# Two of three exponent shifts from DVE to GpSimd, singly allotted shift buffers, a packed output projection and one query map, in a statically scheduled attention kernel

## The chip, the cores and the metric

The kernel runs on one core of one Trainium2 chip. The metric is device time in microseconds (us); for the profiled run of the kernel before it was 802.34 us, 1.8 us more than the span from the first to the last instruction that its profile shows. One core has PE (TensorE, matmuls), DVE (VectorE), ACT (ScalarE), GpSimd (written POOL in the profile) and SP, which here only starts DMA transfers. "Clock" is the mean TensorE clock that the profile shows as granted, as a share of full speed. Runs that are more than 1.5% slower than the fastest of the same kernel are marked slow; the ratios below use only the fast ones.

## The reference

Two independent layers share the launch; the outputs lie side by side.

```python
# A: multi-query attention, S=2048, D=512, H=32 heads of Dh=16, one shared key and value head
q = (x @ wq) as [H, S, Dh];  k = x @ wk;  v = x @ wv
p = softmax(q @ k.T * Dh**-0.5);  a = concat_heads(p @ v) @ wo
# B: linear attention
q, k, v = x @ wqkv, by head
phi(t) = concat(softmax(t @ w_phi), softmax(-(t @ w_phi)))     # per head
o = (phi(q) @ (phi(k).T @ v)) / (phi(q) @ sum(phi(k)) + 1e-6);  b = o @ wo
out = concat(a, b, axis=-1)
```

What matters is the exponential in A: 32 heads x 2048 x 2048 scores. In blocks of 128 keys by 512 queries, four of which make a "quad", that is 512 quads. Two engines can turn a quad of scores in PSUM into exponentials, and both are used at once.

## The kernel before

The first way is ACT: `exp` out of PSUM, two or three blocks at a time. The second is DVE, which builds the exponential out of float16 bits. One instruction per block (a "conversion") scales the score and writes it as int16, so that the bits, read as float16, are a rough power of two. Three more copies of the quad are this one plus 256, 512 and 768 (the "shifts": 256 is a quarter of an exponent step). PE then sums all four copies, each with its own weight K in the value matrix VK; the weighted sum is a better exponential.

```python
# kernel before, cut
def bits():                       # "dz": one of 4 blocks of a quad, PSUM -> SBUF
    o = Z[:, 0, h, :]             # Z: 3 quad buffers x 4 copies x 4 blocks x 512, int16
    v.tensor_scalar(out=o, in0=ps[:, bank, :], scalar1=self.Z1, scalar2=self.Z0, op0=ALU.mult, op1=ALU.add)
def shift(t):                     # "dS": t = 1, 2, 3, all on DVE
    v.tensor_scalar(out=Z[:, t], in0=Z[:, 0], scalar1=256.0 * t, scalar2=None, op0=ALU.add)
def d_pv(quad):                   # "dpv": one PE job of 16 matmuls, after all three shifts
    for k in range(4):
        for g in range(4):
            pe.matmul(ps[32 * g:32 * g + 32, bank, :], lhsT=w[:, k, :], rhs=Zf[:, k, sl[g], :],
                      start=start and k == 0, stop=stop and k == 3, tile_position=(0, 32 * g))
```

The order of instructions on every engine is fixed before launch. A planner on the host lists jobs with durations measured earlier, issues the job that can start first, and thereby fixes each engine's queue and how many quads DVE takes. On the chip the engines are held together only by semaphores, and a semaphore is set only where one instruction reads or overwrites data of another. The planner decides freely how many quads DVE takes. It also puts filler matmuls on constant data into PE gaps when its count of recent PE activity is low.

```python
def weight(self, j):              # PE activity of a job, cut
    if j.mode == "row": return 0.28 * (self.gsize[j.name[1]] if k == "qk" else 1)
    if j.mode == "col": return 0.41 if k == "kv" else 0.68 if k == "pv" else 2.7     # 2.7: "dpv", 16 matmuls
# in run(): if n >= 2 and te > 14 and self.active(s) < self.ACTIVE: ... issue a filler
```

Of the kernel before, what the change touches and what calls it, by code (L numbers as in the profile page):

```python
# [1159 lines left out]
class _Fast:  # L1160
# [13 lines left out]
    NQ = 3  # L1174

    def __init__(self, nc, st, ins, out):
# [22 lines left out]
        self.Z = sb("Z", [128, self.NQ, 4, 4, 512], I16)  # L1199
        self.onesK = sb("onesK", [128, 4, 32], BF)  # L1200
        self.bmx = sb("bmx", [128, 64], F32)
        self.On = sb("On", [128, 12, 512], BF)
        self.wo_pad = sb("wo_pad", [128, 8, 512], BF)
# [10 lines left out]
        self.Wq = sb("Wq", [128, 4, 2, 16, 2, 16], BF)  # L1214
# [4 lines left out]
        self.Ek = sb("Ek", [128, 2, 32, 2, 16], BF)  # L1219
        self.vS = sb("vS", [128, 2, 32, 2, 17], BF)  # L1220
# [4 lines left out]
        self.KVs = sb("KVs", [128, 8, 2, 2, 4], BF)  # L1225
# [17 lines left out]
        self.fin = 0.0  # L1243
# [50 lines left out]
    def ready(self, j):  # L1294

        if j.keys is None:
            self.rec = []
            j.fn()
            j.keys = ({r for _, rs, _ in self.rec for r in rs}, {w for _, _, ws in self.rec for w in ws if w != ("PS", None)})
            self.rec = None  # L1300
        t = j.rel
        rs, ws = j.keys
        for m, kk in ((self.tw, rs | ws), (self.tr, ws)):
            for k in kk:
                if k in m:
                    f, e = m[k]
                    if e != j.eng:
                        f += self.SEM
                    elif e == "pe":
                        f = 0.0  # L1310
                    t = max(t, f)
        if j.nb:
            fr = sorted(max(self.tr.get(("PS", b), (0.0,))[0], 0.0) + self.SEM for b in self.free)
            if len(fr) < j.nb:
                return None
            t = max(t, fr[j.nb - 1])
        return t

    def issue(self, j, start):
# [11 lines left out]
        self.te[j.eng] = max(self.te[j.eng], start + dur)  # L1331
        self.fin = start + dur + self.TAIL[j.eng]
# [78 lines left out]
    def head(self):  # L1411
# [23 lines left out]
        for k in range(4):  # L1435
            add("pool", (lambda k: (lambda g: g.memset(self.VK[:, k, :, 16:32], self.K[k])))(k), writes=[("VK1", k)])
            add("pool", (lambda k: (lambda g: g.memset(self.onesK[:, k, :], self.K[k])))(k), writes=["onesK"])
        add("pool", lambda g: g.memset(self.denS, 1.0), writes=[("denS", 0), ("denS", 1)])
        add("pool", lambda g: g.memset(self.bmx, 0.0), writes=["bmx"])
        if True:  # L1440
# [10 lines left out]
            add("pool", lambda g: g.memset(self.wo_pad, 0.0), writes=["wo_pad0"])  # L1451
            S.batch_begin("sp")
            for g in range(4):
                for e in range(2):
                    srcw = self.A_wo.rearrange("(A g e d) n -> g e d A n", A=4, g=4, e=2)[g, e]
                    dstw = self.wo_pad[32 * g:32 * g + 16, e:8:2, :]
                    S.dma((lambda s_, d_: (lambda q: q.dma_start(d_, s_)))(srcw, dstw), reads=["wo_pad0"], writes=["wo_pad"])
            S.batch_end()
# [11 lines left out]
            for a in range(2):  # L1470
                o = self.KVs[:, :, 0, a, :]
                add("pool", (lambda a, o: (lambda g: g.tensor_copy(out=o, in_=mask[:, 1 - a, :].unsqueeze(1).to_broadcast([128, 8, 4]))))(a, o),
# [9 lines left out]
        for k, t in (("wk_rep", 3.5), ("half1", 3.0), ("wv", 8.2), ("wq", 8.2), ("VA1", 5.0), ("ones", 1.0), ("zero", 1.0), ("bmx", 14.0)):  # L1482
# [11 lines left out]
    def jobs_a(self):  # L1494
# [16 lines left out]
        for qt in range(12):  # L1511
            qc = qt // 4
            for h in range(2):
                job(("op", qt, h), "pe", 0.87, (lambda qt, h: (lambda: self.outproj(qt, h)))(qt, h), mode="full", nb=1 - h, prio=3.5 - 2.6 * h,
                    after=[("on", qc * 8 + a) for a in range(4 * h, 4 * h + 4)] + ([("op", qt, 0)] if h else [("on", qc * 8 + 7)]))
            job(("oa", qt), "dve", 0.60, (lambda qt: (lambda: self.outproj2(qt)))(qt), after=[("op", qt, 1)], frees=[("op", qt, 0)], prio=1)
        for i in range(4):
            for h in range(2):
                job(("pp", i, h), "pe", 0.87 if h == 0 else 0.44, (lambda i, h: (lambda: self.out_part(i, h)))(i, h), mode="full", nb=1 - h, prio=3.5 - 2.6 * h,
                    after=[("on", 24 + a) for a in range(6)] + [("bk", 15), ("bv", 15)] + [("bq", 3, G) for G in range(8)] + ([("pp", i, 0)] if h else []))  # L1520
            job(("ppc", i), "dve", 0.60, (lambda i: (lambda: self.out_part2(i)))(i), after=[("pp", i, 1)], frees=[("pp", i, 0)], prio=1)
        for sc in range(31):
            job(("rc", sc), "dve", 0.18, (lambda sc: (lambda: self.finish_sc2(sc)))(sc), after=[("ac", sc)], prio=1.1)
            job(("on", sc), "dve", 0.60, (lambda sc: (lambda: self.finish_sc3(sc)))(sc), prio=1.3,
                after=[("rc", sc)] + ([("op", 4 * ((sc - 12) // 8) + i, (sc - 12) % 8 // 4) for i in range(4)] if sc >= 12 else []))
# [136 lines left out]
    def sums(self, sc):  # L1662

        start, stop = self.ndone[sc] == 0, self.ndone[sc] == 15
        if self.rec is None:
            self.ndone[sc] += 1
# [9 lines left out]
    def pv(self, q):  # L1676
# [4 lines left out]
        start, stop = self.sums(sc)  # L1681
# [19 lines left out]
    def dq_ok(self):  # L1701
        if self.dbusy > self.DBUSY or self.dz_out >= self.NOUT or self.dn // 4 - self.NQ >= self.dpvq:
            return False
        return self.dn % 4 != 0 or self.dve_quad() is not None

    def next_dq(self):
# [3 lines left out]
        p = quad % self.NQ  # L1710
        Z = self.Z[:, p]

        def scores():
            if self.rec is None:
                if h == 0:
# [3 lines left out]
                    self.dleft = [0, 1, 2, 3]  # L1719
                sc, kap = self.dquads[quad]  # L1720
# [13 lines left out]
        def bits():  # L1734
            bank, ps = self.bank(("dq", k)), self.ps
            o = Z[:, 0, h, :]
            self.add("dve", lambda v: v.tensor_scalar(out=o, in0=ps[:, bank, :], scalar1=self.Z1, scalar2=self.Z0, op0=ALU.mult, op1=ALU.add),  # L1737
                     reads=[("PS", bank)], writes=[("Z", p, h)])
            if self.rec is None:
                self.dz_out -= 1  # L1740
                self.dbusy += 1.2 if h == 3 else -0.6
        self.job(("dq", k), "pe", 0.22, scores, mode="row", nb=1, prio=1.0, ok=self.dq_ok)
        self.job(("dz", k), "dve", 0.60, bits, after=[("dq", k)], frees=[("dq", k)], prio=1.2)
        if h < 3:
            return
        zk = [("Z", p, x) for x in range(4)]

        def shift(t):
            def go():
                self.add("dve", lambda v: v.tensor_scalar(out=Z[:, t], in0=Z[:, 0], scalar1=256.0 * t, scalar2=None, op0=ALU.add),  # L1750
                         reads=zk, writes=[("Zt", p, t)])
                if self.rec is None:
                    self.dbusy -= 0.6
            return go
        for t in range(1, 4):
            self.job(("dS", quad, t), "dve", 0.60, shift(t), after=[("dz", k - x) for x in range(4)], prio=2)
        self.job(("dpv", quad), "pe", 0.87, lambda: self.d_pv(quad), mode="col", prio=1.4,
                 after=[("dS", quad, t) for t in range(1, 4)] + [("va", x) for x in range(4)], ok=lambda: self.acc_ok(self.dquads[quad][0]))

    def d_pv(self, quad):  # L1760
# [3 lines left out]
        p = quad % self.NQ  # L1764
        Zf = self.Z[:, p].bitcast(F16)
        start, stop = self.sums(sc)
        rd = [("VK", k, kap // 4) for k in range(4)] + [("VK1", k) for k in range(4)] + ["onesK"]
        rd += [("Z", p, h) for h in range(4)] + [("Zt", p, t) for t in range(1, 4)]
        todo = [(self.ACC, self.VK[:, :, kap, :])] + ([(self.den_bank, self.onesK)] if sc == 31 else [])
        for bank, w in todo:  # L1770
            def fn(pe, bank=bank, w=w):
                mm = None
                for k in range(4):
                    for g in range(4):
                        mm = pe.matmul(ps[32 * g:32 * g + 32, bank, :], lhsT=w[:, k, :], rhs=Zf[:, k, sl[g], :],  # L1775
                                       start=start and k == 0, stop=stop and k == 3, tile_position=(0, 32 * g))
                return mm
            kw = dict(writes=[("PS", bank)]) if start else dict(accum=[("PS", bank)])
            self.add("pe", fn, reads=sorted(set(rd), key=str), **kw)
        if self.rec is None:  # L1780
            self.dpvq += 1
# [33 lines left out]
    def finish_sc3(self, sc):  # L1815
        r, qc, a = sc % 2, sc // 8, sc % 8
        accS, R, On = self.accS, self.denS, self.On
        self.add("dve", lambda v: v.tensor_tensor(out=On[:, sc % 12, :], in0=accS[:, r, :], in1=R[:, r, :], op=ALU.mult),  # L1818
                 reads=[("accS", r), ("denS", r), ("row", r)], writes=[("On", sc % 12)])

    def outproj(self, qt, half):
# [3 lines left out]
        bank = self.bank(("op", qt, 0))  # L1825
        q0 = (qt % 4) * 128

        def fn(pe):
            mm = None
            for a in range(4 * half, 4 * half + 4):  # L1830
                mm = pe.matmul(ps[:, bank, :], lhsT=On[:, (8 * qc + a) % 12, q0:q0 + 128], rhs=self.wo_pad[:, a, :], start=(a == 0), stop=(a == 7))  # L1831
            return mm
        kw = dict(writes=[("PS", bank)]) if half == 0 else dict(accum=[("PS", bank)])
        self.add("pe", fn, reads=[("On", (qc * 8 + a) % 12) for a in range(4 * half, 4 * half + 4)] + ["wo_pad", "wo_pad0"], **kw)

    def outproj2(self, qt):
        ps, oa = self.ps, self.outA
        bank = self.bank(("op", qt, 0))
# [6 lines left out]
    def out_part(self, i, half):  # L1845
        ps, On = self.ps, self.On
        bank = self.bank(("pp", i, 0))
        lo, hi = (0, 4) if half == 0 else (4, 6)

        def fn(pe):  # L1850
            mm = None
            for a in range(lo, hi):
                mm = pe.matmul(ps[:, bank, :], lhsT=On[:, a, i * 128:i * 128 + 128], rhs=self.wo_pad[:, a, :], start=(a == 0), stop=(a == 5))
            return mm
        kw = dict(writes=[("PS", bank)]) if half == 0 else dict(accum=[("PS", bank)])
        self.add("pe", fn, reads=[("On", a) for a in range(lo, hi)] + ["wo_pad", "wo_pad0"], **kw)

    def out_part2(self, i):
        bank = self.bank(("pp", i, 0))
        self.copy(self.part[:, i, :], self.ps[:, bank, :], [("PS", bank)], [("part", i)] + [("BxT", c) for c in range(4)])  # L1860

    def finish_last(self):
# [8 lines left out]
        def last(i, a):  # L1871
            def fn(pe):
                return pe.matmul(ps[:, i, :], lhsT=self.On[:, a, i * 128:i * 128 + 128], rhs=self.wo_pad[:, a, :], start=(a == 6), stop=(a == 7))
# [483 lines left out]
```

## Time and profile before

The kernel took 797.5 us (median of the first three runs) and 800.25 us with one run more. The profiled run spans 800.5 us.

The table of busy time, kernel before: busy us, share of the span, number of instructions.

```profile
PE 754.1 (94%) x7457; PEld 246.6 (31%) x7457; DVE 727.9 (91%) x1261; ACT 746.9 (93%) x688; POOL 17.2 (2%) x49
```

The costliest groups, kernel before: line, engine, operation, output<-input, shapes and count, then busy us in total, mean ns of one, and idle time just before.

```profile
L1645 ACT ACTIVATE f_PT<-f_ps 128x1536 bf16<-128x1536 f32 x619 | 719.5, 1262 | 36.4 <-PE f_ps L1590 33.0
L1737 DVE TENSOR_SCALAR f_Z<-f_ps 128x512 int16<-128x512 f32 x500 | 326.6, 681 | 28.5 <-PE f_ps L1590 28.1
L1750 DVE TENSOR_SCALAR f_Z<-f_Z 128x2048 int16<-128x2048 int16 x375 | 247.8, 684 | 1.1
L1396 PE MATMUL f_ps<-f_ones,f_zero 128*128 128x512 bf16 (+9 forms) x229 | 65.9, 354 | 2.0 <-POOL f_zero L1415 1.3
```

ACT's exponentials (L1645), DVE's conversions (L1737) and shifts (L1750) fill their two engines; GpSimd is empty. 500 conversions are 125 quads on DVE; the other 387 are ACT's. The last line is the fillers, matmuls on constant data that the planner puts into PE gaps.

### The profile page before, as it was taken

To read this page: it belongs to the slowest core of one execution; us is meant where nothing else is said; L and a number is where in the kernel's file an instruction comes from. 1 tells how busy PE (TensorE), PEld (TensorE's weight loads), DVE (VectorE), ACT (ScalarE), POOL (GpSimd) and SP (SyncE) were. 2 spreads that over 40 slices of the span, in tenths; PEclk is the share of its full clock that TensorE was granted. 3 is DMA by queue.
4 is the path that set the end of the run, shared out by engine and by line. 5 is a ranking of instruction groups with operands and counts; after the bars stand their busy time and mean duration, and the time that the engine had idled before them with its cause. 6 is when DMAs were issued, how large, how long until landed. Compare 5 with 4: busy or idle time off the path is not lost.

```text
span 800.5 us, 17448 instructions
## 1 busy us (share of the span) xinstructions
PE 754.1 (94%) x7457; PEld 246.6 (31%) x7457; DVE 727.9 (91%) x1261; ACT 746.9 (93%) x688; POOL 17.2 (2%) x49
## 2 busy tenths in 40 slices
PE   8999999999999999999999999999999999989995
PEld 2323222333233233333333333333223333333332
DVE  3799999999899999997989898999899989999954
ACT  3999998999899999999999999999899999999972
POOL 5000000000000000011000000000000000000000
PEclk9999999999799999999999999999899999999999
DMA  6561111110111110111101111110111111011111
GB/s 133 111 129 9 9 7 8 8 8 4 6 8 21 22 8 4 7 9 8 9 4 19 35 7 9 21 15 10 6 9 21 22 21 19 11 9 15 21 14 37
DMA packets 45181, 17.12 MB, mean 21 GB/s; under 512 B 37092, under 2 KB 43236, under 8 KB 45096
## 3 DMA queue, kind: packets, MB, share of 16 engines
q1 hardware_dynamic: 45096, 15.93, 16.0%
q8 instruction: 60, 0.98, 0.5%
q14 instruction: 25, 0.20, 0.1%
HBM read 2.15 MB, written 4.19 MB: 8 GB/s over the span
## 4 chain that ended last, share of the span: by engine, by line
DVE 64%; PE 26%; ACT 4%; DMA 3%; SPq 2%; issue 1%; POOL 0%; DVEq 0%; POOLq 0%
DVE f_Z L1737 26%; DVE f_Z L1750 19%; PE f_ps L1590 8%; PE f_ps L1775 4%; PE f_ps L1687 4%; ACT f_PT L1645 4%; PE f_ps L2084 3%; DVE f_vS L2033 2%; DVE f_ssum L2007 2%; PE f_ps L1396 2%; DVE f_On L1818 2%; DVE f_Wk L2144 2%; DVE f_accS L1402 2%; PE f_ps L1831 1%; DMA f_denS<-f_denS 1%
## 5 line engine op out<-in xcount | busy, mean ns | idle before, releaser
L1645 ACT ACTIVATE f_PT<-f_ps 128x1536 bf16<-128x1536 f32 x619 | 719.5, 1262 | 36.4 <-PE f_ps L1590 33.0
L1737 DVE TENSOR_SCALAR f_Z<-f_ps 128x512 int16<-128x512 f32 x500 | 326.6, 681 | 28.5 <-PE f_ps L1590 28.1
L1590 PE MATMUL f_ps<-f_QA,f_KR 32*128 32x512 bf16 x2048 | 314.4, 389 | 24.2 <-DVE f_Z L1737 13.5
L1750 DVE TENSOR_SCALAR f_Z<-f_Z 128x2048 int16<-128x2048 int16 x375 | 247.8, 684 | 1.1
L1590 PEld LDWEIGHTS f_ps<-f_QA,f_KR 32*128 32x128 bf16 x2048 | 80.1, 91 | 256.0 <-ACT f_PT L1645 87.9
L1687 PE MATMUL f_ps<-f_PT,f_VA 128*32 128x512 bf16 x1548 | 152.5, 393 | 0.7 <-DVE f_accS L1402 0.2
L1775 PE MATMUL f_ps<-f_Z,f_VK 128*32 128x512 f16 x2000 | 133.3, 387 | 3.7 <-DVE f_Z L1750 1.7
L1396 PE MATMUL f_ps<-f_ones,f_zero 128*128 128x512 bf16 (+9 forms) x229 | 65.9, 354 | 2.0 <-POOL f_zero L1415 1.3
L1687 PEld LDWEIGHTS f_ps<-f_PT,f_VA 128*32 128x32 bf16 x1548 | 38.1, 93 | 93.5 <-issue 82.7
L1775 PEld LDWEIGHTS f_ps<-f_Z,f_VK 128*32 128x32 bf16 x2000 | 42.9, 96 | 64.5 <-DVE f_Z L1750 14.3
L2084 PE MATMUL f_ps<-f_BxT,f_Wq 128*128 128x512 bf16 x128 | 33.2, 382 | 1.6 <-DVE f_Z L1737 1.0
L1396 PEld LDWEIGHTS f_ps<-f_ones,f_zero 128*128 128x128 bf16 (+2 forms) x229 | 17.7, 97 | 33.2 <-issue 21.7
L1831 PE MATMUL f_ps<-f_wo_pad,f_On 128*128 128x512 bf16 x96 | 24.9, 382 | 0.6 <-DVE f_Z L1737 0.6
L2144 DVE TENSOR_TENSOR f_Wk<-f_ps,f_wq 128x512 bf16<-128x512 f32 x32 | 21.7, 681 | 2.7 <-PE f_ps L2133 2.7
L1818 DVE TENSOR_TENSOR f_On<-f_accS,f_denS 128x512 bf16<-128x512 f32 x31 | 21.2, 682 | 1.3 <-DMA f_denS<-f_denS 1.2
L1402 DVE COPY f_accS<-f_ps 128x512 f32<-128x512 f32 x31 | 21.2, 684 | 1.1 <-PE f_ps L1687 1.0
L2091 ACT ACTIVATE f_ET<-f_ps 128x512 bf16<-128x512 f32 x32 | 20.8, 649 | 0.6 <-PE f_ps L2084 0.5
L1542 DVE TENSOR_SCALAR f_KR<-f_ps,f_half 128x512 bf16<-128x512 f32 x8 | 5.6, 746 | 15.8 <-PE f_ps L1534 15.8
L2033 DVE TENSOR_TENSOR f_vS<-f_ps,f_rs 128x1024 bf16<-128x1024 f32 x16 | 19.6, 1222 | 0.0
L2001 ACT ACTIVATE f_Ek<-f_ps 128x512 bf16<-128x512 f32 x32 | 17.7, 622 | 1.8 <-PE f_ps L1993 1.7
L2007 DVE TENSOR_REDUCE f_ssum<-f_Ek 128x64 f32<-128x1024 bf16 x16 | 19.4, 1212 | 0.0
L2174 PE MATMUL f_ps<-f_Bwo,f_oT 128*128 128x512 bf16 x64 | 16.6, 382 | 2.2 <-DVE f_Z L1737 1.2
(95 smaller groups left out, 325.9 us busy)
## 6 DMA issues: line engine op xcount, KB each, us to landing
f_denS<-f_denS SPq DMA_DIRECT2D x124, 30.0 KB, 3.0
out_dram<-f_outB SPq DMA_DIRECT2D x18, 128.0 KB, 1.9
f_denC<-f_accS SPq DMA_DIRECT2D x124, 2.0 KB, 1.7
f_denS<-f_denC SPq DMA_DIRECT2D x124, 2.0 KB, 1.7
out_dram<-f_outA SPq DMA_DIRECT2D x14, 128.0 KB, 2.2
f_wq<-in_A_wq_dram SPq DMA_DIRECT2D x1, 512.0 KB, 4.0
f_Bwv<-in_B_wqkv_dram SPq DMA_DIRECT2D x1, 512.0 KB, 5.3
f_Bwo<-in_B_wo_dram SPq DMA_DIRECT2D x1, 512.0 KB, 9.3
```

Source lines behind the costliest of these rows:

```text
L1396: mm = pe.matmul(ps[0:m, bank, 0:n].rearrange("p (a n) -> p a n", n=128), lhsT=zero[0:r, 0:m], rhs=rhs, start=start, stop=start, **kw)
L1402: self.add("dve", lambda v: v.tensor_copy(out=out, in_=in_), reads=reads, writes=writes)
L1590: return pe.matmul(self.ps[:, bank, :], lhsT=self.KR[32 * g:32 * g + 32, sc % 2, kap * 128:(kap + 1) * 128], rhs=self.QA[32 * g:32 * g + 3 ...
L1645: self.add("act", lambda a: a.activation(out=PT[:, sl[0]:sl[0] + size, :], in_=ps[:, b0:b0 + size, :], func=ACT.Exp), reads=[("PS", b0 + i ...
L1687: mm = pe.matmul(ps[32 * g:32 * g + 32, bank, :], lhsT=w, rhs=PT[:, slots[g], :], start=start, stop=stop, tile_position=(0, 32 * g))
L1737: self.add("dve", lambda v: v.tensor_scalar(out=o, in0=ps[:, bank, :], scalar1=self.Z1, scalar2=self.Z0, op0=ALU.mult, op1=ALU.add), reads ...
L1750: self.add("dve", lambda v: v.tensor_scalar(out=Z[:, t], in0=Z[:, 0], scalar1=256.0 * t, scalar2=None, op0=ALU.add), reads=zk, writes=[("Z ...
L1775: mm = pe.matmul(ps[32 * g:32 * g + 32, bank, :], lhsT=w[:, k, :], rhs=Zf[:, k, sl[g], :], start=start and k == 0, stop=stop and k == 3, t ...
L1818: self.add("dve", lambda v: v.tensor_tensor(out=On[:, sc % 12, :], in0=accS[:, r, :], in1=R[:, r, :], op=ALU.mult), reads=[("accS", r), (" ...
L2033: self.add("dve", lambda v: v.tensor_tensor(out=vS[:, :, :, 0:16], in0=v3, in1=rs.unsqueeze(3).to_broadcast([128, 32, 2, 16]), op=ALU.mult ...
L2084: mm = pe.matmul(ps[:, bank, :], lhsT=w[:, dc].rearrange("p x h a f -> p (x h a f)")[:, G * 128:G * 128 + 128], rhs=xT[:, dc, m * 512:(m + ...
L2144: self.add("dve", lambda v: v.tensor_tensor(out=o, in0=i, in1=w.unsqueeze(3).to_broadcast([128, 2, 16, 16]), op=ALU.mult), reads=[("PS", b ...
```

## The change

Its intent is to free DVE. Two of the three shifts of a quad go to GpSimd, as int32 adds of two packed int16 values. The Z memory is the same size but allotted as 12 single copies instead of 3 quads, and the quad's product on PE is split into four jobs, one for each copy. The planner treats the access of GpSimd adds, DVE shifts ("dS") and DVE output scalings ("on") to the on-chip memory SBUF as one resource, which this text calls the port: it plans no GpSimd add while a shift or a scaling is planned, nor the reverse. On PE, the output projection is packed to half the matmuls by a DMA that moves odd heads to free partitions, and B's query map is computed once and exponentiated with both signs. The diff, cut; `...` marks what is left out:

```diff
-        self.Z = sb("Z", [128, self.NQ, 4, 4, 512], I16)          # NQ = 3
+        self.Z = sb("Z", [128, self.NZ, 4, 512], I16)             # NZ = 12
+        self.step = sb("step", [128, 2, 2], I16)                  # 512, 512 and 768, 768
@@ ready(), issue(): the shared port as a resource of the plan
+        if j.eng == "pool" or j.name[0] in self.LOCK:
+            t = max(t, self.te_port)
...
+        if j.eng == "pool" or j.name[0] in self.LOCK:
+            self.te_port = start + dur
@@ shifts
-                self.add("dve", lambda v: v.tensor_scalar(out=Z[:, t], in0=Z[:, 0], scalar1=256.0 * t, scalar2=None, op0=ALU.add),
-                         reads=zk, writes=[("Zt", p, t)])
+                if eng == "dve":
+                    fn = lambda v: v.tensor_scalar(out=Z[:, z], in0=Z[:, z0], scalar1=256.0 * t, scalar2=None, op0=ALU.add)
+                else:
+                    a, b = (Z[:, x].rearrange("p h n -> p (h n)").bitcast(I32) for x in (z0, z))
+                    c = self.step[:, t - 2, :].bitcast(I32).to_broadcast([128, 1024])
+                    fn = lambda g: g.tensor_tensor(out=b, in0=a, in1=c, op=ALU.add)
+                self.add(eng, fn, reads=zk, writes=[("Z", z)] + [("Zp", z, x) for x in range(4)])
+        for t in (3, 2, 1):
+            left = max(self.te["pool"] - self.fin, 0.0) + self.PSHIFT * self.pooled
+            eng = "pool" if t > 1 and left < self.PLEFT[3 - t] else "dve"
@@ the product: one job for each copy
-        self.job(("dpv", quad), "pe", 0.87, lambda: self.d_pv(quad), mode="col", prio=1.4,
-                 after=[("dS", quad, t) for t in range(1, 4)] + ...)
+        for t in range(4):
+            self.job(("dpv", quad, t), "pe", 0.22 if sc < 31 else 0.43, ... self.d_pv(quad, t) ..., mode="col", prio=1.4,
+                     after=([("dS", quad, t)] if t else []) + ...)
+    PSHIFT = 1.95
+    PLEFT = (4.0, 2.0, 0.0)
+    LOCK = ("dS", "on")
@@ output projection, odd heads moved by DMA; 4 matmuls instead of 8
+        if r:
+            for g in range(4):
+                dst = self.On[32 * g + 16:32 * g + 32, p % 6, :] ...   # <- self.Ot, 16 partitions
-            for a in range(4 * half, 4 * half + 4):
+            for A in range(4):
@@ query map: half the matmuls, two exponentials each
-    def b_eq(self, m, G):
-        ... activation(out=self.ET[:, sl, :], in_=self.ps[:, bank, :], func=ACT.Exp)
+    def b_eq(self, m, G, a):
+        ... activation(out=self.ET[:, sl, :], in_=self.ps[:, bank, :], func=ACT.Exp, scale=1.0 - 2.0 * a)
... (layouts of Ek, vS, KVn, KVs follow; the function weight() is not touched)
```

## The prediction

> **What bounds it now.** Three engines share one softmax and all are full. The table of busy time gives PE 754.1 us (94%), ACT 746.9 (93%), DVE 727.9 (91%), GpSimd 17.2 (2%) of 800.5. In the table of stretches ACT and DVE are 95-99% busy from 60 to 760 us. Of 512 score quads, ACT takes 387 (719.5 us in the groups, 1.86 us each) and DVE 125. A DVE quad costs four bit conversions out of PSUM (326.6 us) and three 128x2048 int16 shifts (247.8 us): 4.6 us. The chain of waits is 45% these two DVE lines. PE is near its limit but not at it: about 58 us of its busy time between 20 and 780 us are filler matmuls on ones and zeros.
>
> **What changes.** Two of three shifts go to GpSimd as 128x1024 int32 adds. A DVE quad falls to about 3.3 us (4 x 0.653 + 0.661). Balance: ACT 1.86(512-n) + 27 = DVE 3.27n + 151 + about 15 of port waits gives n near 158 quads on DVE, about 685 us on each, against 747/728. The 53 us during which ACT is not busy (mostly the first and last 20 us) stay: ideally 738 us.
>
> PE: one query map saves 64 matmuls (half of 33.2 us), packed output projection about half of 24.9 + 6.6 + 2.1 us: some 33 us busy. About 33 more DVE quads cost PE 12 more matmuls each (about 0.65 us, from 16 in 0.87 us), some 21 us. So PE work is about level, in less time: fillers shrink, PE waits take part of the gain. ACT work for the query map is unchanged. Four more transfers per pair of heads lie off the chain (DMA share about 12%).
>
> **What it may cost.** GpSimd time of one add: no such instruction is in this trace; the change's planner says 1.95 us; the 2-input add in the skill's table (GPSIMD Engine Reference, Performance versus the Vector engine: 4497 ns for 2048) halves to an estimate of 2.25 us. SBUF — State Buffer, "Who interferes with whom", says a GpSimd instruction and a DVE instruction in a 2-port mode, or with two SBUF inputs, exclude each other. The port then carries about 2 x 1.95 + 0.66 = 4.6 us per quad, over 700 us for 158 quads: nearly full. The plan models this for shifts and output scaling, so some shifts stay on DVE (I expect 1.7-1.9 per quad on GpSimd), but not for the small SBUF-only DVE instructions (about 40). No run here shows this yet. Expected loss over ideal: 10-25 us.
>
> **Prediction: 757 us, 80% range 738 to 788; faster by over 2% 0.82, within 2% 0.13, slower 0.05.**
>
> **What would show it.** Bit conversions rise from 500 to 600-650; exponentials fall from 619 to about 575 at the same 1.26 us mean; DVE shifts fall from 375 to 160-210; GpSimd shows 260-310 adds of about 2 us, busy 70-80%; query-map matmuls 128 to 64, output projection 96 to 48; ACT and DVE still over 90%, PE too. Port conflict would show as DVE shifts with mean well over 0.68 us, small SBUF-only DVE instructions likewise, and waits of PE and DVE on GpSimd adds.
>
> **What would make it wrong.** If an add takes 2.3 us or more, the static order lags behind GpSimd and everything waits on it: time near 790-800. If port blocking is smaller and PE follows well, 740. If splitting the quad's product into four PE jobs adds many row/column mode switches, PE becomes the bound, with DVE and ACT idle on PE scores: 770-785.

## More of the kernel before

A small DVE instruction that will matter, in the groups kept apart by shape:

```profile
L2013 DVE TENSOR_TENSOR f_bmx<-f_ssum,f_bmx 128x64 f32<-128x64 f32 x16 | 3.6, 222 | 0.0
```

The times of the plan are not enforced.

## The result, and the profile after

The changed kernel took 883.12 us (median of 4; the two fast runs 872.56 and 879.45, the two slow ones 886.79 and 891.49), against 800.25 us for the kernel before. The ratio of the fast runs is 1.0948 (95% interval 1.0827 to 1.1069): 9.5% slower. All ratios in this document are the mean time of one kernel's fast runs over that of the kernel before's fast runs of the same rounds, so not quite the ratio of the medians that are quoted.

The table of busy time, changed kernel (span 877.7 us, clock 0.909; before it was 0.981):

```profile
PE 783.3 (89%) x7351; PEld 233.4 (27%) x7351; DVE 729.4 (83%) x1094; ACT 736.8 (84%) x674; POOL 471.7 (54%) x277
```

The groups that answer to those of before, and the small DVE instruction:

```profile
L1650 ACT ACTIVATE f_PT<-f_ps 128x1536 bf16<-128x1536 f32 x605 | 706.5, 1254 | 118.0 <-PE f_ps L1595 111.1
L1778 POOL TENSOR_TENSOR f_Z<-f_Z,f_step 128x1024 int32<-128x1024 int32 x226 | 458.4, 2028 | 387.6 <-DVE f_Z L1749 360.3
L1749 DVE TENSOR_SCALAR f_Z<-f_ps 128x512 int16<-128x512 f32 x536 | 350.5, 683 | 74.0 <-PE f_ps L1595 71.9
L1773 DVE TENSOR_SCALAR f_Z<-f_Z 128x2048 int16<-128x2048 int16 x176 | 180.4, 1048 | 0.5
L1402 PE MATMUL f_ps<-f_ones,f_zero 128*128 128x512 bf16 (+7 forms) x139 | 43.5, 384 | 1.9 <-POOL f_zero L1421 1.3
L2054 DVE TENSOR_TENSOR f_bmx<-f_ssum,f_bmx 128x64 f32<-128x64 f32 x16 | 11.4, 710 | 0.0
```

Three things stand out. DVE does 199 shifts fewer (136 us at 0.684), yet is busy as long as before (729.4 us): each of the 176 remaining shifts takes 1.048 us instead of 0.684 (64 us more), there are 36 conversions more (24 us), and small instructions grew, as L2054 from 0.222 to 0.710 us. The conversions, which read PSUM, still take 0.683 us. And ACT, whose own work shrank, now waits 111 us for scores from PE, where it waited 33.

The third is the clock. In the busy-by-stretch table, changed kernel (columns: stretch and its length in us; PE, PEld, DVE, ACT, POOL busy us and counts, granted clock, DMA share, GB/s):

```profile
100.00:200.00 100.00, 85.68 (x886) 24.51 (x882) 90.41 (x127) 81.27 (x75) 55.30 (x27) 0.88 0.11 8
500.00:600.00 100.00, 96.26 (x954) 33.97 (x950) 85.72 (x137) 96.62 (x93) 61.76 (x32) 1.00 0.13 16
```

Where ACT is starved (81 us busy of 100) the clock is low too; where the engines keep step (500 to 600 us) it is full. In the other stretches of 100 us between 200 and 800 us ACT was busy for 85 to 89 us, at a clock of 0.83 to 0.93. The records of the clock hold only two values, 0.5 and 1.0: 162 us at 0.5 in 19 stretches, against 32 us in 6 for the kernel before. In the 3.5 us before each of the 19, PE stood idle for 51% of the time on average, against about 10% overall. Groups of score matmuls at a granted clock of 0.50 and of 1.00 (PE timeline, changed kernel; columns: start us, duration us, engine, line, operation; `xN` is N merged instructions, [idle before]):

```profile
101.30 0.61 PE L1595 MATMUL f_ps<-f_QA,f_KR 32*128 32x512 bf16 x3
210.05 0.39 PE L1595 MATMUL f_ps<-f_QA,f_KR 32*128 32x512 bf16 x3
```

The planner's own timetable, read out on the host, is useful beside this. It is no measurement, only the plan to which the queues were laid:

```
                end of plan   PE      of it fillers   ACT     DVE     quads on DVE   GpSimd adds
kernel before   785.4 us      764.0   45.6            763.6   720.5   125            0
changed kernel  766.4 us      752.9   26.7            746.7   620.3   134            226
```

The plan hoped for 19 us. The kernel before ran about 15 us over its plan, the changed one about 115.

A first look at single waits, as timelines of one engine. Changed kernel, DVE, then GpSimd:

```profile
210.18 0.68 DVE L1749 TENSOR_SCALAR f_Z<-f_ps 128x512 int16<-128x512 f32 x1
210.78 0.68 DVE L1860 TENSOR_TENSOR f_Ot<-f_accS,f_denS 128x512 bf16<-128x512 f32 x1
211.38 2.38 DVE L1773 TENSOR_SCALAR f_Z<-f_Z 128x2048 int16<-128x2048 int16 x1
```

```profile
210.94 4.57 POOL L1778 TENSOR_TENSOR f_Z<-f_Z,f_step 128x1024 int32<-128x1024 int32 x2 [2.38 <-DVE f_Z L1749]
```

The conversion ends at 210.86 and completes a quad. The GpSimd adds of that quad start 0.08 us later. But the plan had put first the scaling (L1860), then the shift (L1773), then these adds, 1.2 us after the conversion (an extract of the plan; columns: start us, duration us, engine, job):

```
179.36  0.60  DVE     dz 123      conversion that completes quad 30
179.96  0.60  DVE     on 5        output scaling
180.56  0.60  DVE     dS 28, t=2  shift
181.16  1.95  GpSimd  dS 30, t=3  add
183.11  1.95  GpSimd  dS 30, t=2  add
```

Nothing in the program holds the add to its planned place: its only inputs are the conversions. It takes the port early, and the DVE shift takes 2.38 us instead of 0.68. Every later instruction in DVE's queue is 1.7 us late. Of all 176 DVE shifts in the trace of the changed kernel, 51 took over 0.1 us more than 0.684, the largest cluster (33) by 1.5 to 1.75 us, and together 64 us; none waited longer than one add takes. Set beside the queues of the plan, 32 of the 51 (53 of the 64 us) had been overtaken by an add that was planned after them, as here; the other 19 ran into an add that was planned before them and was still running.

### The profile page after: what moved, and what is told of

Same layout as the page of the kernel before. It is cut to its first block, busy times and chain, and to the rows that moved or that the text cites. A ratio compares the mean times of both kernels' runs of the same rounds, so it can differ in the third digit from the quotient of the medians.

```text
span 877.7 us, 17512 instructions
## 1 busy us (share of the span) xinstructions
PE 783.3 (89%) x7351; PEld 233.4 (27%) x7351; DVE 729.4 (83%) x1094; ACT 736.8 (84%) x674; POOL 471.7 (54%) x277
## 4 chain that ended last, share of the span: by engine, by line
PE 51%; DVE 37%; ACT 6%; POOL 2%; issue 2%; DMA 1%; SPq 1%; DVEq 0%; POOLq 0%
PE f_ps L1595 19%; PE f_ps L1809 13%; DVE f_Z L1749 12%; DVE f_Z L1773 12%; PE f_ps L1692 9%; ACT f_PT L1650 5%; DVE f_accS L1408 2%; DVE f_vS L2074 1%; DVE f_Ot L1860 1%; PE f_ps L2217 1%; PE f_ps L1402 1%; PE f_ps L2034 1%; PE f_ps L2064 1%; DVE f_ssum L2048 1%; DVE f_On L1860 1%
## 5 line engine op out<-in xcount | busy, mean ns | idle before, releaser
L1778 POOL TENSOR_TENSOR f_Z<-f_Z,f_step 128x1024 int32<-128x1024 int32 x226 | 458.4, 2028 | 387.6 <-DVE f_Z L1749 360.3
L1749 DVE TENSOR_SCALAR f_Z<-f_ps 128x512 int16<-128x512 f32 x536 | 350.5, 683 | 74.0 <-PE f_ps L1595 71.9
L1595 PE MATMUL f_ps<-f_QA,f_KR 32*128 32x512 bf16 x2048 | 338.6, 412 | 32.6 <-DVE f_Z L1749 14.3
L1809 PE MATMUL f_ps<-f_Z,f_VK 128*32 128x512 f16 x2144 | 208.3, 420 | 29.4 <-DVE f_Z L1773 17.7
L1773 DVE TENSOR_SCALAR f_Z<-f_Z 128x2048 int16<-128x2048 int16 x176 | 180.4, 1048 | 0.5
L1402 PE MATMUL f_ps<-f_ones,f_zero 128*128 128x512 bf16 (+7 forms) x139 | 43.5, 384 | 1.9 <-POOL f_zero L1421 1.3
L1585 PE MATMUL f_ps<-f_AxT,f_wq 128*128 128x512 bf16 x64 | 18.1, 410 | 1.8 <-DVE f_Z L1749 1.7
L2034 PE MATMUL f_ps<-f_Wk,f_BxT 128*128 128x512 bf16 x64 | 19.0, 426 | 0.8 <-DVE f_Z L1749 0.8
L2064 PE MATMUL f_ps<-f_Bwv,f_BxT 128*128 128x512 bf16 x64 | 19.4, 432 | 0.0
L2125 PE MATMUL f_ps<-f_BxT,f_Wq 128*128 128x512 bf16 x64 | 17.4, 397 | 0.0
```

Source lines behind the costliest of these rows:

```text
L1402: mm = pe.matmul(ps[0:m, bank, 0:n].rearrange("p (a n) -> p a n", n=128), lhsT=zero[0:r, 0:m], rhs=rhs, start=start, stop=start, **kw)
L1595: return pe.matmul(self.ps[:, bank, :], lhsT=self.KR[32 * g:32 * g + 32, sc % 2, kap * 128:(kap + 1) * 128], rhs=self.QA[32 * g:32 * g + 3 ...
L1749: self.add("dve", lambda v: v.tensor_scalar(out=o, in0=ps[:, bank, :], scalar1=self.Z1, scalar2=self.Z0, op0=ALU.mult, op1=ALU.add), reads ...
L1773: fn = lambda v: v.tensor_scalar(out=Z[:, z], in0=Z[:, z0], scalar1=256.0 * t, scalar2=None, op0=ALU.add)
L1778: fn = lambda g: g.tensor_tensor(out=b, in0=a, in1=c, op=ALU.add)
L1809: mm = pe.matmul(ps[32 * g:32 * g + 32, bank, :], lhsT=w, rhs=Zf[:, sl[g], :], start=start, stop=stop, tile_position=(0, 32 * g))
```

## The experiments

Three theories were held against each other. Port: GpSimd adds and DVE shifts exclude each other, DVE falls behind the plan, and PE, ACT and the clock follow. Clock: the split made each quarter of a product count 2.7 in `weight()`, four times too much for a quad, so the planner puts in too few fillers (27 us planned instead of 46) and the TensorE clock drops. The third was that GpSimd itself, 1.9 us for one shift, is too slow for the products that wait for it.

All runs below had three timed rounds and one profiled run; they also ran the kernel before on the same chip. All give the right result unless stated.

### weight: count PE activity right

```diff
-            return 0.41 if k == "kv" else 0.68 if k == "pv" else 2.7
+            return 0.41 if k == "kv" else 0.68 if k in ("pv", "dpv") else 2.7
```

> The changed kernel, with the planner's count of PE activity mended: a quarter of a quad's product counts 0.68 instead of the 2.7 that was right for the whole quad, so the plan puts in more filler matmuls (planned 36 us instead of 27). Clock theory (the miscount starves the PE clock of activity and it is halved in stretches): clock above 0.97, 770 to 800 us. Port theory (GpSimd adds and DVE shifts exclude each other, DVE falls behind the plan, all the rest follows from that): clock still about 0.91, DVE shifts still about 1.0 us on average, 855 to 885 us.

Measured: 886.39 us, ratio 1.1021 (1.0907 to 1.1135), clock 0.895. The groups by shape:

```profile
L1773 DVE TENSOR_SCALAR f_Z<-f_Z 128x2048 int16<-128x2048 int16 x173 | 172.0, 1017 | 1.9 <-PE f_ps L1809 1.0
```

The port theory's shifts and clock came, with the median time 1 us above its band; the miscount is real but is not the cause.

### before_count4: put the miscount into the kernel before

```diff
-            return 0.41 if k == "kv" else 0.68 if k == "pv" else 2.7
+            return 0.41 if k == "kv" else 0.68 if k == "pv" else 10.8
```

> The kernel before, with the miscount put in on purpose (a quad's product counts 10.8 instead of 2.7); nothing of GpSimd, so no port conflict. Planned fillers 34 us instead of 46. Clock theory: clock falls to about 0.91, 840 to 880 us. Port theory: clock stays at about 0.97 or more, 797 to 808 us.

Measured: 805.38 us, ratio 1.0045 (0.9994 to 1.0096), clock 0.966. The clock theory asked for 840 us or more and fell a second time.

### tinypool: the same queues, GpSimd adds of 16 columns

```diff
-                    fn = lambda g: g.tensor_tensor(out=b, in0=a, in1=c, op=ALU.add)
+                    fn = lambda g: g.tensor_tensor(out=b[:, 0:16], in0=a[:, 0:16], in1=c[:, 0:16], op=ALU.add)
```

Z is also set once at the start, so that nothing unwritten is read. A comparison of the programs shows the same instructions in the same order on PE, ACT, DVE and SP. The result is wrong.

> The changed kernel with the same order of instructions on every engine and the same waits, but each GpSimd add covers 16 of 1024 columns (wrong result on purpose). Port theory: DVE shifts fall to 0.68 us and the time to 775 to 800 us, the clock back to about 0.97 by itself, with the miscount still there. Clock theory: DVE shifts fall to 0.68 us as well, but the fillers are still too few, the clock stays below 0.94 and the time above 840 us.

Measured: 784.28 us, ratio 0.9765 (0.9698 to 0.9832), clock 0.957 in the profiled run (0.957 to 0.976 in all four). In the groups by shape, this run:

```profile
L1773 DVE TENSOR_SCALAR f_Z<-f_Z 128x2048 int16<-128x2048 int16 x176 | 116.3, 684 | 2.3 <-PE f_ps L1809 1.7
L1778 POOL TENSOR_TENSOR f_Z<-f_Z,f_step 128x16 int32<-128x16 int32 x226 | 74.6, 330 | 669.1 <-DVE f_Z L1749 628.7 <-DVE f_Z L1773 26.8 <-PE f_ps L1809 6.1
```

The shift is back at 0.684 us. With the fillers still too few, the clock came back from 0.909 to 0.957 by itself, on the very same list of PE instructions: the low clock was a consequence of the delays. The length of the adds costs 1.0948 - 0.9765 = 0.118 of about 800 us, some 95 us. This run can't say whether by the port or by GpSimd's slowness; the next one can.

### reduce: full adds, but reductions in place of the DVE shifts

```diff
-                    fn = lambda v: v.tensor_scalar(out=Z[:, z], in0=Z[:, z0], scalar1=256.0 * t, scalar2=None, op0=ALU.add)
+                    fn = lambda v: v.tensor_reduce(out=Z[:, z, 0, 0:1], in_=Z[:, z0, 0, :], axis=AX.X, op=ALU.max)
```

> The changed kernel, same order and same GpSimd adds of full size; each DVE shift is replaced by a reduction of 512 columns, an instruction that takes the same 0.68 us when alone[...] (wrong result on purpose). Port theory (the exclusive port between adds and shifts): these instructions take 0.68 us also beside adds, time near that of the run with tiny adds, 785 to 805 us. Rival, the slow GpSimd itself (2 us a shift is late for the products on PE): time stays at 860 us or more.

Measured: 809.89 us, ratio 1.0087 (1.0023 to 1.0151), result wrong. That is 5 us above the port theory's band, and 50 below the rival's. The groups by shape:

```profile
L1778 POOL TENSOR_TENSOR f_Z<-f_Z,f_step 128x1024 int32<-128x1024 int32 x226 | 432.8, 1915 | 338.1 <-DVE f_Z L1749 312.1 <-DVE f_Z L1773 11.8 <-PE f_ps L1809 1.0
L1773 DVE TENSOR_REDUCE f_Z<-f_Z 128x1 int16<-128x512 int16 x176 | 114.9, 677 | 1.3 <-PE f_ps L1809 0.8
L2054 DVE TENSOR_TENSOR f_bmx<-f_ssum,f_bmx 128x64 f32<-128x64 f32 x16 | 11.2, 697 | 0.0
```

GpSimd does its full work, and the replaced instructions take 0.677 us beside it. So the exclusion between shifts and adds is worth 1.0948 - 1.0087 = 0.086, some 69 us, and the slowness of GpSimd is not the main cause. The rest, 1.0087 - 0.9765 = 0.032 or about 26 us, holds both the conflict of adds with DVE instructions that read SBUF twice (L2054 still 0.697 us, the output scalings 0.90 and 0.96) and the later arrival of the copies; no run separates those two.

### enforce: make the program keep the planned slot

Each GpSimd add also waits for the last DVE shift or scaling that the plan issued before it. Queues and data are otherwise those of the changed kernel; line numbers are 7 higher.

```diff
+        if eng == "pool" and self.held is not None:
+            k["deps"] = [self.held]
         t = self.S.add(eng, fn, reads=reads, writes=writes, accum=accum, **k)
+        if eng == "dve" and self.lock:       # lock: the job being issued is in LOCK
+            self.held = t
```

> The changed kernel with the same order of instructions on every engine and one thing more: each GpSimd add also waits for the DVE shift or output scaling that the plan had put before it on the shared port. Unenforced-slot theory (the plan reserves a slot for a DVE shift between two adds, but nothing in the program keeps the next add from starting, so DVE loses it by a hair and waits a whole add): DVE shifts fall from 1.05 to below 0.80 us on average, time 785 to 820 us. Rival (the port is simply overbooked at 226 adds and 176 shifts, whatever their order): 860 us or more, the waits only move to GpSimd and from there to PE.

Measured: 817.75 us, ratio 1.0150 (1.0070 to 1.0230), profiled run 807.56 us at a clock of 0.962 (with the PE queue of the changed kernel, and a right result). Added waits alone took about 64 us off (1.0948 - 1.0150). The DVE shifts:

```profile
L1780 DVE TENSOR_SCALAR f_Z<-f_Z 128x2048 int16<-128x2048 int16 x176 | 133.4, 781 | 0.5
```

The same place of the plan as shown above, in this run, DVE and then GpSimd:

```profile
186.84 0.68 DVE L1756 TENSOR_SCALAR f_Z<-f_ps 128x512 int16<-128x512 f32 x1
187.44 0.68 DVE L1867 TENSOR_TENSOR f_Ot<-f_accS,f_denS 128x512 bf16<-128x512 f32 x1
188.04 0.68 DVE L1780 TENSOR_SCALAR f_Z<-f_Z 128x2048 int16<-128x2048 int16 x1
```

```profile
188.80 3.86 POOL L1785 TENSOR_TENSOR f_Z<-f_Z,f_step 128x1024 int32<-128x1024 int32 x2 [3.39 <-DVE f_Z L1780]
```

The two adds start after the shift and take 3.86 us together, not 4.57; neither side waits. In the whole trace no shift was overtaken by an add planned after it any more; 33 shifts (17 us together) still ran into an add planned before them, which these waits don't prevent. So what cost most was not that the port was overbooked, but that it was handed out in another order than planned.

### enforce_wl: the small two-input instructions too, and activity counted right

```diff
-    LOCK = ("dS", "on")
+    LOCK = ("dS", "on", "rs", "vs", "qw")     # and weight() as in the run "weight"
```

> As the run with enforced slots, and the other small DVE instructions that read SBUF twice are put under the same rule, and PE activity is counted right (planned fillers 37 us). If slots are what matters: 780 to 810 us, a little below the run with enforced slots, small DVE instructions back at 0.2 to 0.3 us, clock 0.96 or more.

Measured: 802.17 us, ratio 0.9985 (0.9926 to 1.0044), clock 0.977; the small instruction of L2054 (L2061 here) back at 0.292 us. Another 13 us or so, from two edits at once whose shares are not known; they also change the plan (216 adds instead of 226). This is level with the kernel before, still some 35 us over its plan of 766.4 us.

### nopool, nopool_weight, nopool_join: the rest of the change without GpSimd

```diff
-    PLEFT = (4.0, 2.0, 0.0)                   # nopool; nopool_weight: also weight() as above
+    PLEFT = (0.0, 0.0, 0.0)
-    LAST = dict(pe=(80, 16), act=(4, 4), dve=(6, 6), pool=(0, 0), sp=(12, 0))
+    LAST = dict(pe=(32, 16), act=(4, 4), dve=(6, 6), pool=(0, 0), sp=(4, 0))
```

> The changed kernel with all three shifts of a quad on DVE (single buffers, packed projection, one query map, miscount kept; the split of the last instructions around the flag shortened, so that it does not deadlock). The planner's own timetable ends at 774 us, fillers planned 18 us. Port theory: DVE shifts 0.68 us, clock about 0.97, 785 to 805 us. Clock theory: clock about 0.91 or less, 850 us or more.

Measured: 816.86 us, ratio 1.0217 (1.0139 to 1.0295), clock 0.956, DVE shifts 0.680 us. Better than the changed kernel by 7 points, but above what the port theory allowed: something else in the change costs too.

> The changed kernel with no shifts on GpSimd, PE activity counted right: planned fillers 35 us instead of 18. The run without GpSimd and with the miscount took 817 us at a clock of 0.956, 43 us over its plan of 774. If too few fillers explain that: clock 0.975 or more and 785 to 800 us. If the split of a quad's product into four PE jobs or the single buffers explain it: 805 to 820 us again.

Measured: 806.70 us, ratio 1.0072 (1.0016 to 1.0127), clock 0.971. The miscount is worth about 12 us here (1.0217 - 1.0072; by the two intervals, give or take 8); but the kernel still is not below the one before.

`nopool_join` makes the product one PE job again:

```diff
-        for t in range(4):
-            self.job(("dpv", quad, t), "pe", 0.22 if sc < 31 else 0.43, ..., after=([("dS", quad, t)] if t else []) + ...)
+        self.job(("dpv", quad), "pe", 0.87, lambda: [self.d_pv(quad, t) for t in range(4)], mode="col", prio=1.4,
+                 after=[("dS", quad, t) for t in range(1, 4)] + ...)
```

> The changed kernel with no shifts on GpSimd and a quad's product again as one PE job after all three shifts (as the kernel before has it): what is left of the change is the packed projection, the one query map and singly allotted buffers. Planned end 779 us against 785 of the kernel before; 1397 planned mode switches of PE against 1579 with split products. If the split is what makes the run without GpSimd miss its plan by 35 us (the kernel before misses its own by 15): 788 to 797 us. If not: 802 to 812 us.

Measured: 799.12 us, ratio 0.9983 (0.9932 to 1.0033), clock 0.987. Joining the product took about 7 us off (give or take 6), a little short of what was expected, and the time lands 2 us above the expected band. The gap before weight loads of these products points to where the split costs, though weight loads overlap matmuls, so that this idle time is not lost one for one. Groups by line, `nopool_weight` (split) and then `nopool_join`:

```profile
L1809 PEld LDWEIGHTS f_ps<-f_Z,f_VK 128*32 128x32 bf16 x2048 | 47.9, 94 | 117.1 <-issue 46.6 <-DVE f_Z L1773 42.6 <-DVE f_accS L1408 10.5
```

```profile
L1808 PEld LDWEIGHTS f_ps<-f_Z,f_VK 128*32 128x32 bf16 x2000 | 43.5, 96 | 65.6 <-issue 23.0 <-DVE f_accS L1408 5.7 <-DVE f_Z L1773 5.2
```

Split, the weight loader idles 117 us before these products, 43 of them until a DVE shift is done; joined, 66 us and 5. The run also tells what the packed projection, the single query map and the singly allotted buffers are worth together: with them and all shifts on DVE the kernel is level with the one before, although half of two groups of matmuls is gone. There were more fillers instead: 81.2 us of them in this run, 65.9 in the kernel before. Less PE work alone did not shorten the kernel.

### enforce_join and ej_p1: both corrections, with 213 and with 128 adds

`enforce_join` has the enforced slots with the longer LOCK list and the joined product (for which 2.7 is the right weight again). `ej_p1` has in addition `PLEFT = (2.0, 0.0, 0.0)`: one shift a quad on GpSimd.

> Slots on the shared port enforced for all DVE instructions that read SBUF twice or shift, and the quad's product as one PE job; about 1.66 shifts a quad on GpSimd. Planned end 773 us. Both corrections together: 782 to 794 us, below the kernel before. If the port still costs what it did with enforced slots (DVE shifts 0.8 us), about 790; if the split was harmless, 798 to 806.

> As the run with enforced slots and joined product, but one shift a quad on GpSimd (128 adds instead of 213), two on DVE. The planner's timetable ends at the same 773 us, because DVE is not what bounds it. If the remaining port waits matter: DVE shifts below 0.75 us and 3 to 10 us less than with 213 adds. If they do not: the same within 3 us.

Measured: `enforce_join` 787.75 us, ratio 0.9810 (0.9756 to 0.9865), clock 0.975; `ej_p1` 795.72 us, ratio 0.9928 (0.9881 to 0.9974). `enforce_join` is correct and beats both kernels: 1.9% below the one before, clear of noise, but not surely by 2%. Its groups (line numbers moved):

```profile
L1785 POOL TENSOR_TENSOR f_Z<-f_Z,f_step 128x1024 int32<-128x1024 int32 x213 | 403.1, 1892 | 342.9 <-DVE f_Z L1780 168.6
L1780 DVE TENSOR_SCALAR f_Z<-f_Z 128x2048 int16<-128x2048 int16 x171 | 139.6, 844 | 0.5
L1657 ACT ACTIVATE f_PT<-f_ps 128x1536 bf16<-128x1536 f32 x615 | 708.8, 1272 | 35.2 <-PE f_ps L1602 33.0
```

ACT waits 33.0 us for PE, as in the kernel before, and about half of the time in which GpSimd waits for its adds it now waits for DVE's shifts, as the plan wants. For `ej_p1`, the shifts:

```profile
L1780 DVE TENSOR_SCALAR f_Z<-f_Z 128x2048 int16<-128x2048 int16 x256 | 182.9, 744 | 0.8
```

The expectation for `ej_p1` was wrong in both its forms: shifts do get shorter with fewer adds (0.744 us against 0.844), yet the kernel is 8 us slower. With 0, 128 and 213 adds the joined kernel takes 799, 796 and 788 us (the first of these without the enforced slots, which without shifts on GpSimd would hardly bind). So moving shifts to GpSimd does pay, in spite of the plan's saying 772.9 and 772.6 us for the last two. Why it pays more than the plan says stays open.

## Why the prediction was wrong

The prediction was 757 us with a range of 738 to 788; the kernel took 883.

- **Right:** the kind of costs. A DVE quad got cheaper in shifts, the adds took about the planner's time (1.892 us undisturbed, not the estimated 2.25), query-map and projection matmuls were halved, and the prediction named the signs by which a port conflict would be known: DVE shifts well over 0.68 us and small SBUF-only instructions likewise. Both came (1.048 us; L2054 0.710 us). PE's own waits for adds, a part of the third sign, came to only 11 us.
- **The step that failed, first term:** "The plan models this for shifts and output scaling ... Expected loss over ideal: 10-25 us." A resource that the planner models is not one that the program keeps. The adds had no reason to wait for the DVE instruction that was planned before them, started 0.08 us after their last input, and took the port. Measured, the length of the adds cost about 95 us, of which some 69 belong to the exclusion between shifts and adds; extra waits alone gave back 64, and with them no shift was overtaken any more.
- **Second term, the ideal of 738 us:** it balanced ACT against DVE and found 158 quads for DVE. The plan gave DVE only 134 (536 conversions, and 226 adds instead of the expected 260 to 310), with DVE busy 620 of 766 us and ACT and PE full in its own timetable. In the plan DVE was not the scarce engine that the sum took it for. What freeing it brings was measured in two ways: with adds cut to 0.33 us the changed kernel, split and miscount still in it, took 784 us, 46 above the ideal; and with both corrections, 213 adds instead of none brought about 14 us (0.9983 to 0.9810), not 60. The prediction noted that a DVE quad costs PE 12 more matmuls, but did not put PE into the balance.
- **Third term, the PE savings:** "some 33 us busy" was taken as an offset for more DVE quads. Without shifts on GpSimd and without the split they bring nothing measurable (ratio 0.9983): there were more fillers instead.
- **Named only as a risk:** splitting the product. Between the nearest pairs it costs about 7 us without GpSimd (1.0072 to 0.9983) and about 14 us with enforced slots (0.9985 to 0.9810), each give or take some 6. The second pair differs only in the split and in the weights that go with it, and so in the plan (216 and 213 adds).
- **Not foreseen:** the miscount in `weight()`. It costs about 12 us without shifts on GpSimd, and nothing visible in the changed kernel.
- **The clock:** it fell to 0.909 in the changed kernel. The Trainium skill (TensorE: Matmul & The Clock Gate, "What's actually happening") says that the clock gate follows how busy PE has recently been. The trace agrees: the clock fell to half after stretches in which PE had waited (51% idle, against 10% overall), groups of score matmuls lengthened there from about 0.39 to 0.61 us, and shorter adds alone bring the clock to 0.957 with the same PE queue. How many of the 95 us went by way of the clock was not separated. An estimate from the two profiled runs: the clock withheld 877.7 x (1 - 0.909) = 80 us from the changed kernel and 788.3 x (1 - 0.957) = 34 us from the run with short adds, so its direct share is at most about 46 of the 89 us between their spans.

## What to carry to other kernels

In a statically ordered kernel, a resource that two engines exclude each other from should be given out by semaphores, in the order of the plan (worth 64 us here); a slot that only the planner knows of is lost to whichever engine is released first, and then everything queued behind the loser is late. Before counting what an offload frees, see whether the freed engine is the scarce one in the plan itself, and put every engine into the balance. When a job is split, look for the tables that count it: a weight per job is wrong by the factor of the split.

## What the Trainium skill lacked or had wrong

- SBUF — State Buffer, "Who interferes with whom", was right in what excludes what: a DVE shift from SBUF to SBUF went from 0.684 to up to 2.42 us beside adds, a two-input DVE instruction from 0.222 to 0.710 us on average, while conversions from PSUM (0.683 us) and reductions (0.677 us) were untouched. It says that issue order decides who waits; it lacks how close this can be: an add that started 0.08 us after its input ended kept a DVE shift, planned before it, waiting for 1.7 us.
- GPSIMD Engine Reference, "Performance versus the Vector engine": the table's 4497 ns for 2048 fp32 elements would give an estimate of about 2.25 us for 1024. The 128x1024 int32 add with a repeated second operand took 1.892 us, and three in a row 5.90 us. No page gives a time for this case.
- TensorE: Matmul & The Clock Gate: no page has a measured case in which a delay between two other engines reaches the clock of a kernel that keeps PE busy with fillers. Here the clock went from 0.957 to 0.909 with the same PE queue, when 226 GpSimd adds were lengthened from 0.33 to 2.03 us.
